# Four paired groups (two chunks of one batch each) instead of two, with a new order of work, in a linear-attention kernel with a feed-forward layer behind it

## The chip, the cores and the metric

The kernel runs on one core of one Trainium2 chip. The metric is the device time of one execution in microseconds (us), lower is better. The core has five engines that work side by side and meet only at semaphores: TensorE (PE; its weight loads are listed as PEld), VectorE (DVE), ScalarE (ACT), GpSimd (POOL) and SyncE (SP), which here does nothing but issue DMA. Data moves between HBM and SBUF (128 partitions) through 16 DMA engines, which all queues share. Matmuls write PSUM, which has 8 banks here taken two at a time as four slots.

## The reference

Two layers, one behind the other. The first is a linear attention with a state that decays; the second a feed-forward layer whose activation is a smoothed relu:

```python
# r, k, v: [4 batches, 8 heads, 768 tokens, 48];  w, u: [8, 48]
for t in range(S):
    cur = einsum('bhd,bhe->bhde', u * k[t], v[t])
    y[t] = einsum('bhd,bhde->bhe', r[t], state + cur)
    state = w * state + einsum('bhd,bhe->bhde', k[t], v[t])
x = y as [3072 tokens, 384]
h = x @ w_in                      # [3072, 2048]
g = where(h >= 1, h, where(h <= -1, 0, (h + 1)**2 / 4))
out = g @ w_out                   # [3072, 384], float32
```

## The kernel before

The 768 tokens of a batch are cut into 6 chunks of 128. The work comes in 12 **groups** of 256 tokens. Before, a group is one chunk of two batches: group g has chunk g // 2 of batches 0, 1 (g even) or 2, 3 (g odd). Two layouts exist (`PAIRED`, line 22). A **plain** group (2 to 11) has one token in each of the 128 partitions, and the two batches stand one behind the other in the free dimension; a load of its R, K or V is one DMA whose pieces are 48 numbers, 192 bytes (line 212). A **paired** group (0 and 1) has one batch in partitions 0 to 63 and the other in 64 to 127, two neighbouring tokens in a partition; its pieces are 96 numbers, 384 bytes, and a load is two DMAs of 64 partitions each (lines 203 to 207).

What one group goes through, by the names of its steps:

- `ldR`, `ldK`, `ldV`: the loads, 384 KB each; SP issues them, or ACT where the step says `@A`.
- `Rs`, `Ks` (line 289): R and K times a table of powers of w, in bf16. `T`, `TT` transpose the result on TensorE and copy it out of PSUM (for groups below `T_BY_DMA`); for the others `RK` (line 343) does it as a DMA transpose on SP's queue.
- `A` (the products of K and R within a chunk), `AT` (times a causal mask), `Vc` (V in bf16), `Y` (A times V, plus the state times R when there is an earlier chunk).
- `KU`, `RU`, `us`, `ud`: the token's own term with u, and `y`, its sum with Y.
- `Sp`, `Tm`, `dc`, `sb`: the chunk's share of the state, its sum with the old state, the decay, and the state's bf16 copy for the next chunk.
- `X`, `xT`: y transposed, on TensorE (groups below `X_BY_DMA`) or by a DMA transpose on SP's queue (line 475).
- `up` q (q = 0 to 3): 12 matmuls for a quarter of the hidden layer; `re`, `sq` on ACT and `ga` on VectorE are its activation; `dn` j, q: the matmuls of the second product for half j of the group; `o` and `st` copy it out of PSUM and store it.
- Once: `wu`, `wd`, `vu`, `vd` (tables), `wi`, `wo` (each half of w_in and w_out, issued by POOL and cast to bf16 by the DMA), `kw` n (n matmuls on zeros), `mk` (line 267, a DMA that reads the end of w_in and writes a few bytes, so SP's queue waits there for w_in).

The order is written out by hand, or rather by a search, as one list (`ORDER`, lines 29 to 65). A step with `@A`, `@D` or `@P` runs on ACT, VectorE or POOL, `#n` names the PSUM slot. The loop at line 530 issues the steps in the order of the list; each engine runs its own in that order, and an engine whose next instruction must wait holds back all that stand behind it. Work tiles have a fixed number of buffers (line 99): three each for R, K and V, two for o, KU and RU.

## Time and profile before

| | us |
|---|---|
| median of 2 runs | 206.17 (205.96 to 206.37) |
| profiled execution, its own time | 205.72 |
| its span | 203.9 |
| TensorE busy | 170.5 |
| VectorE busy | 153.8 |
| ACT busy | 126.0 |
| POOL busy | 104.1 |

The page tells busy time per engine and, in 40 slices of the span, how busy each was. The windows give the same for any stretch, with TensorE's granted clock, the share that the DMA engines were busy (above 1 where transfers overlap within an engine) and GB/s moved. The chain of waits follows the work that ended last back to its start. The timeline lists instructions with the idle time of their engine before them and what ended it.

### The profile page before, as it was taken

What the parts mean: (1) busy time and instruction counts of PE and PEld (TensorE: products, weight loads), DVE (VectorE), ACT (ScalarE), POOL (GpSimd) and SP (SyncE); (2) the same over time, 40 slices, a digit from 0 to 9 for tenths busy, and PEclk for the clock granted to TensorE, in tenths of its full rate; (3) what the DMA queues carried; (4) which work ended last, traced back from release to release, by engine and by line L of the source; (5) the groups of instructions that cost most, each with busy time, mean ns of one, the idle gap of its engine ahead of it and who ended that gap; (6) DMA issues with size and microseconds to landing.
All of it is one profiled execution on the core that took longest, in us unless ns stands there. A gap on an engine that the chain in (4) does not pass through costs nothing.

```text
span 203.9 us, 4261 instructions
## 1 busy us (share of the span) xinstructions
PE 170.5 (84%) x1780; PEld 126.5 (62%) x1780; DVE 153.8 (75%) x155; ACT 126.0 (62%) x142; POOL 104.1 (51%) x76
## 2 busy tenths in 40 slices
...
DMA  4999999993099999999999989962704710332004
GB/s 94 210 207 221 169 194 203 165 204 43 7 202 187 151 240 149 238 186 197 152 255 192 228 182 193 216 150 51 141 3 89 219 30 0 102 21 77 3 0 154
DMA packets 100452, 29.19 MB, mean 143 GB/s; under 512 B 94544, under 2 KB 99408, under 8 KB 100432
## 3 DMA queue, kind: packets, MB, share of 16 engines
...
q10 hardware_dynamic: 1056, 0.39, 0.9%
...
q14 instruction: 6, 0.05, 0.1%
HBM read 20.84 MB, written 4.72 MB: 125 GB/s over the span
## 4 chain that ended last, share of the span: by engine, by line
PE 39%; DMA 27%; DVE 9%; POOL 9%; SPq 5%; issue 5%; ACT 4%; DVEq 0%; POOLq 0%; ACTq 0%
PE hp L482 17%; PE op L504 15%; DMA V<-in_v_dram 9%; DMA RKT<-RK 7%; DMA R<-in_r_dram 6%; DMA K<-in_k_dram 5%; POOL RK L289 4%; DVE gt L497 3%; DVE KU L298 3%; SPq L207 2%; POOL RU L304 2%; PE A L366 2%; POOL V L317 1%; DVE RK L289 1%; SPq L212 1%
## 5 line engine op out<-in xcount | busy, mean ns | idle before, releaser
L482 PE MATMUL hp<-xT,w_in_sb 128*128 128x256 bf16 x576 | 72.0, 280 | 9.6 <-DVE gt L497 5.9
L489 ACT ACTIVATE pt<-hp 128x1024 f32<-128x1024 f32 x48 | 48.8, 1019 | 39.1 <-PE hp L482 38.9
L504 PE MATMUL op<-w_out_sb,gt 128*128 128x384 bf16 x384 | 69.5, 326 | 4.0 <-DVE o L117 2.5
L482 PEld LDWEIGHTS <-w_in_sb 128*128 128x128 bf16 x576 | 56.8, 100 | 21.8 <-issue 10.3
L497 DVE SCALAR_TENSOR_TENSOR gt<-sq,hp 128x1024 bf16<-128x1024 f32 x48 | 57.8, 1214 | 13.0 <-ACT sq L493 12.9
L493 ACT ACTIVATE sq<-pt 128x1024 f32<-128x1024 f32 x48 | 50.5, 1057 | 5.4 <-DVE gt L497 4.1
L504 PEld LDWEIGHTS <-gt 128*128 128x128 bf16 x384 | 35.7, 98 | 25.9 <-issue 4.1
L317 POOL TENSOR_TENSOR V<-Vb,us 128x768 f32<-128x768 bf16 (+1 forms) x11 | 14.9, 1364 | 38.7 <-DVE us L310 23.4
L378 DVE TENSOR_TENSOR AT<-A,mask 128x1024 bf16<-128x1024 f32 x20 | 24.1, 1218 | 6.9 <-PE A L366 6.9
L304 POOL TENSOR_TENSOR RU<-R,KU 128x768 f32<-128x768 f32 (+1 forms) x11 | 20.6, 1873 | 0.3
L298 POOL TENSOR_TENSOR KU<-K,u_bc 128x768 f32<-128x768 f32 (+1 forms) x9 | 14.7, 1636 | 11.8 <-DMA K<-in_k_dram 11.8
L289 POOL TENSOR_TENSOR RK<-R,W 128x768 bf16<-128x768 f32 x9 | 16.7, 1858 | 6.7 <-DMA R<-in_r_dram 6.7
L289 POOL TENSOR_TENSOR RK<-K,W 128x768 bf16<-128x768 f32 x9 | 17.4, 1932 | 2.8 <-DMA K<-in_k_dram 2.8
L329 PE MATMUL T<-ident,RK 128*128 128x128 bf16 x48 | 6.1, 293 | 9.5 <-ACT RKT L117 5.3
L412 POOL TENSOR_TENSOR state<-Tm,wCm 128x768 f32<-128x768 f32 x6 | 10.9, 1821 | 5.0 <-DVE Tm L405 5.0
L460 DVE TENSOR_TENSOR y<-Y,V 128x768 bf16<-128x768 f32 (+1 forms) x13 | 11.5, 888 | 1.7 <-PE Y L440 0.9
L310 DVE TENSOR_REDUCE us<-RU 128x16 f32<-128x768 f32 (+1 forms) x13 | 11.4, 881 | 1.0 <-POOL RU L304 1.0
L298 DVE TENSOR_TENSOR KU<-K,u_bc 128x768 f32<-128x768 f32 x4 | 9.8, 2445 | 2.3 <-DMA K<-in_k_dram 2.3
L117 ACT COPY o<-op 128x384 f32<-128x384 f32 x16 | 7.1, 480 | 7.1 <-PE op L504 7.1
L329 PEld LDWEIGHTS <-RK 128*128 128x128 bf16 x48 | 4.5, 131 | 11.0 <-issue 5.3
L117 ACT COPY RKT<-T 128x1024 bf16<-128x1024 bf16 x5 | 5.1, 1011 | 9.5 <-PE T L329 9.5
L366 PE MATMUL A<-RKT 48*128 48x128 bf16 x160 | 7.6, 218 | 3.6 <-DMA RKT<-RK 2.2
...
## 6 DMA issues: line engine op xcount, KB each, us to landing
...
```

What stands on the lines that cost most here:

```text
L117: nc.scalar.copy(out, in_) if e == "A" else engines[e].tensor_copy(out, in_)
L289: engines[e].tensor_mul(RK[g % NB][:, x, :, hs, :D], rows(got(what, g), g)[:, :, hs], table(x, g, hs))
L298: engines[e].tensor_mul(got("KU", g)[:, :, hs], rows(got("K", g), g)[:, :, hs], u_row)
L304: engines[e].tensor_mul(got("RU", g)[:, :, hs], rows(got("R", g), g)[:, :, hs], got("KU", g)[:, :, hs])
L317: engines[e].tensor_mul(got("V2", g)[:, :, hs], got("Vb", g)[:, :, hs], sums)
L366: nc.tensor.matmul(A[:, i, p, :], t[ps, 1, h, p], t[ps, 0, h, p], start=True, stop=True)
L378: nc.vector.tensor_mul(t.rearrange("p i n t -> p (i n) t"), got("A", g, h).rearrange("p i n t -> p (i n) t"), mask)
L482: nc.tensor.matmul(hp[:, f].rearrange("p (j t) -> p j t", j=2), w_in_sb[:, i, n0 : n0 + P], got("xT", g)[:, :, i, :], start=(i == 0), stop ...
L489: nc.scalar.activation(t, got("hp", g, q), AF.Relu, bias=0.5, scale=0.5)
L493: nc.scalar.activation(t, got("pt", g, q), AF.Square)
L497: nc.vector.scalar_tensor_tensor(out=t, in0=got("sq", g, q), scalar=1.0, in1=got("hp", g, q), op0=ALU.min, op1=ALU.max)
L504: nc.tensor.matmul(got("op", g)[:, j, :DO], got("gt", g, q)[:, f, j * P : (j + 1) * P], w_out_sb[:, n, :], start=(n == 0), stop=(n == nF - 1),
```

## The change

- `PAIRED` becomes groups 0 to 3, and a paired group is something else: **chunks 0 and 1 of one batch** (group g is batch g), chunk 0 in partitions 0 to 63, chunk 1 in 64 to 127, two tokens per partition as before. A load is one DMA into 128 partitions with 384-byte pieces. Groups 4 to 11 are what they were.
- Within a paired group chunk 1 needs the state of chunk 0: `Ta` (VectorE) and `sa` (a copy) make it between Sp and Y, and Y has 8 more matmuls. `Tm`, `dc`, `sb` of these groups work on one batch, half the size.
- Groups 2 and 3 have 16 + 16 short matmuls in A and 64 in Y, as groups 0 and 1 have now. Group 3 is transposed on TensorE instead of by DMA (`T_BY_DMA`, `X_BY_DMA` 3 to 4).
- The store of groups 0 to 3 is one DMA instead of two.
- R0 and K0 are both issued by ACT; `mk` is gone from the list; the whole list is new. POOL has 11 KU (9 before), 9 RU (11), 10 Ks (9), 9 dc (6), 6 sb (0) and one sa; VectorE 2 KU (4), 4 RU (2), 3 Ks (4), 1 dc (2) and 4 Ta; ACT 4 sb (10), 3 sa, 18 o (16).

SP's new list begins: ub, ldK1, ldR1, ldV0, ldR2, ldK2, ldV1, ldV2, ldR3, ldK3, ldK4, ldV3, ldK5, ldR4, ldV4, ldR5, ldV5, RK4, RK5, st0. Of the old list and of the new one the diff shows the first lines.

```diff
--- before.py
+++ after.py
@@ -19,49 +19,51 @@
 
 
 
-PAIRED = (0, 1)
+
+PAIRED = (0, 1, 2, 3)
 
 HALVED = (0,)
-T_BY_DMA, X_BY_DMA = 3, 3
+T_BY_DMA, X_BY_DMA = 4, 4
 
 
 
 ORDER = """
-ub ldK0@A tb ln lp wu0 wu1 wd1 kw21#0 lc#0 wd0 vu ldR0 Rs0.0@D KU0.0@P Ks0.0@D KU0.1@P ldK1 kw14#1 T0.0#1 ldR1 Rs0.1@D
-RU0.0@D ldV0 ldV1 Ks0.1@D wi0 us0.0 vd RU0.1@P wc kw10#0 T0.1#2 TT0.0@A TT0.1@A A0.0#3 Rs1@D Ks1@P wi1 Vc0@A Vc1@A
-ud0.0@P kw10#0 A0.1#0 T1.0#1 us0.1 ud0.1@P Sp0#2 AT0.0 Y0.0#3 AT0.1 Y0.1#0 KU1@P wo0 y0.0 y0.1 TT1.0@A Tm0 T1.1#1 mk0
-TT1.1@A kw3#3 X0#3 xT0@D A1.0#0 RU1@P A1.1#2 up0.0#1 re0.0 sq0.0 AT1.0 AT1.1 Sp1#3 us1 ud1@P Tm1 up0.1#0 Y1#2 up0.2#3
-re0.1 sq0.1 ldK2 ga0.0 up0.3#1 re0.2 sq0.2 ldR2 y1 wo1 X1#2 ga0.1 dn0.0.0#0 dn0.0.1 xT1@D up1.0#2 re0.3 ga0.2 up1.1#3
-sq0.3 KU2@D re1.0 dn0.1.0 dn0.1.1 ldK3 RU2@D sq1.0 ga0.3 ga1.0 re1.1 Rs2@P sq1.1 up1.2#1 us2 Ks2@P T2.0#2 TT2.0@D
...
+ldR0@A ldK0@A tb ln lp wu0 wu1 wd1 kw26#0 lc#0 wc vu wd0 Rs0.0@D Rs0.1@P Ks0.0@D Ks0.1@D kw10#1 T0.0#1 TT0.0@A ub
+KU0.0@P RU0.0@D us0.0 T0.1#2 TT0.1@A ldK1 KU0.1@P RU0.1@D ldR1 Rs1@D Ks1@P wi0 wi1 kw14#0 A0.0#3 AT0.0 ldV0 Vc0@A ldR2
+ud0.0@D ldK2 KU1@D ldV1 ldV2 kw11#0 T1.0#0 Sp0#1 Ta0 us0.1 Tm0 vd T1.1#2 TT1.0@A sa0@A TT1.1@A A0.1#3 A1.0#0 AT0.1
+AT1.0 Y0.0#1 y0.0 Rs2@P Ks2@P kw12#2 T2.0#2 Y0.1#3 A1.1#0 T2.1#1 TT2.0@A A2.0#2 ud0.1@D y0.1 X0#3 ldR3 AT1.1 AT2.0 wo0
+Vc1@A TT2.1@A Sp1#0 A2.1#1 RU1@P KU2@P ldK3 ldK4 Ta1 Tm1 dc0@P xT0@A up0.0#3 Vc2@A ldV3 RU2@P us1 ldK5 ldR4 sa1@A
+dc1@P sb0@A re0.0 sq0.0 ldV4 ldR5 Sp2#2 Ta2 Tm2 up0.1#0 AT2.1 ga0.0 Y1#2 up0.2#1 sa2@A re0.1 sq0.1 sb1@A ud1@P y1 X1#3
+Rs3@P us2 re0.2 sq0.2 xT1@D up0.3#2 re0.3 up1.0#3 ga0.1 ga0.2 Ks3@P T3.0#0 TT3.0@D sq0.3 ga0.3 Y2#1 ud2@P y2 re1.0
+sq1.0 ga1.0 up1.1#0 dc2@P wo1 A3.0#2 AT3.0 re1.1 sq1.1 ga1.1 X2#1 up1.2#3 xT2@A KU3@P T3.1#2 TT3.1@D Vc3@P Sp3#1 Ta3
+Tm3 re1.2 sq1.2 ga1.2 up1.3#0 re1.3 sq1.3 KU4@P sb2@P A3.1#2 AT3.1 ga1.3 up2.0#1 re2.0 sq2.0 up2.1#3 re2.1 sq2.1 RU3@P
+us3 ga2.0 dn0.0.0#2 dn0.1.0 sa3@P Y3#0 dc3@P Vc4@A sb3@A dn0.1.1 up2.2#1 RU4@P ud3@P y3 X3#0 dn0.0.1 ga2.1 xT3@D Rs4@D
+us4 KU5@P RU5@D up2.3#3 up3.0#0 dn0.0.2 dn0.1.2 dn0.0.3 dn0.1.3 re2.2 sq2.2 ga2.2 us5 dn1.0.0#1 dn1.1.0 ldV5 dn1.0.1
...
+st11.1
 """
 
 
@@ -184,6 +186,15 @@
         return x.rearrange("p h d -> p (h d)")
 
 
+    def place(g):
+
+        if g in PAIRED:
+            return 0, g // 2, []
+        if g < 4:
+            return g - 2, 1, [2] if g > 2 else []
+        c, bp = 2 + (g - 4) // 2, g % 2
+        return c, bp, [g - 2] if c > 2 else [2 * bp, 2 * bp + 1] if 2 * bp in PAIRED else [3]
+
     def heads(g, part):
 
         if part is None:
@@ -197,26 +208,21 @@
     def table(i, g, hs):
         return W2[i][:, :, hs] if g in PAIRED else W1[i][:, hs].unsqueeze(1).to_broadcast([P, 2, hs.stop - hs.start, D])
 
-    def load(queue, tile_, x, g, part):
-        c, bp = divmod(g, BP)
-        hs, _ = heads(g, part)
-        if g in PAIRED:
-            for i in range(2):
-                src = x[bp * 2 + i, hs, c * C : (c + 1) * C, :].rearrange("h (q e) d -> q h (e d)", e=2)
-                dst = tile_[i * HP : (i + 1) * HP].rearrange("p (h e) d -> p h (e d)", e=2)[:, hs]
-                queue.dma_start(out=dst, in_=src)
-        else:
-            src = x[bp * 2 : bp * 2 + 2, hs, c * C : (c + 1) * C, :].rearrange("b h t d -> t b h d")
-            dst = tile_.rearrange("p (b h) d -> p b h d", b=2)[:, :, hs]
-            assert part is None
-            queue.dma_start(out=tile_, in_=src.rearrange("t b h d -> t (b h) d"))
+    def load(queue, tile_, x, g):
+        c, bp, _ = place(g)
+        if g in PAIRED:
+            src = x[g, :, : 2 * C, :].rearrange("h (p e) d -> p h (e d)", e=2)
+            queue.dma_start(out=tile_.rearrange("p (h e) d -> p h (e d)", e=2), in_=src)
+        else:
+            src = x[bp * 2 : bp * 2 + 2, :, c * C : (c + 1) * C, :]
+            queue.dma_start(out=tile_, in_=src.rearrange("b h t d -> t (b h) d"))
 
 
     def step_tb(e, s):
         nc.scalar.preload_act_table_set("natural_log_exp_and_others")
 
     def step_ub(e, s):
-        nc.sync.dma_start(out=u_bc, in_=bcast(u))
+        (nc.scalar if e == "A" else nc.sync).dma_start(out=u_bc, in_=bcast(u))
 
     def step_ln(e, s):
         nc.scalar.activation(lw, w_bc, AF.Ln)
@@ -264,7 +270,7 @@
         nc.gpsimd.dma_start(out=w_out_sb[:, n, :], in_=w_out_src[:, n, :])
 
     def step_mk(e, s, i):
-        nc.sync.dma_start(out=mark, in_=(w_in_sb[:1, nK - 1, DF - 16 :],)[i])
+        nc.sync.dma_start(out=mark, in_=w_in_sb[:1, 0, :16])
 
     def step_kw(e, s, n):
         t = bank(s, "idle", (), [P, P], F32)
@@ -272,10 +278,8 @@
             nc.tensor.matmul(t, warm, warm, start=True, stop=True, skip_group_check=True)
 
     def loader(what, x):
-        def step(e, s, g, part=None):
-            if heads(g, part)[1]:
-                new(what, (g,), [P, 2 * H, D], F32)
-            load(nc.scalar if e == "A" else nc.sync, got(what, g), x, g, part)
+        def step(e, s, g):
+            load(nc.scalar if e == "A" else nc.sync, new(what, (g,), [P, 2 * H, D], F32), x, g)
 
         return step
 
@@ -397,25 +401,37 @@
                         flat(got("Vb", g)[:, j, hs, :]), start=True, stop=True, skip_group_check=True,
                     )
 
+    def state_of(g, x):
+        c, bp, _ = place(g)
+        return x[bp][:, g % 2] if g in PAIRED else x[bp]
+
+    def step_Ta(e, s, g):
+        nc.vector.tensor_mul(flat(state_of(g, states)), got("Sp", g)[:, 0, :DM], flat(wCm))
+
+    def step_sa(e, s, g):
+        copy(e, state_of(g, states_bf), state_of(g, states))
+
     def step_Tm(e, s, g):
-        c, bp = divmod(g, BP)
         Sp = got("Sp", g)[:, :, :DM]
-        if c:
+        S = state_of(g, states)
+        if g in PAIRED:
+            t = new("Tm", (g,), [P, NP, 2 * D], F32)
+            nc.vector.tensor_add(flat(t), Sp[:, 1], flat(S))
+        elif place(g)[2]:
             t = new("Tm", (g,), [P, 2, NP, 2 * D], F32)
-            nc.vector.tensor_add(t.rearrange("p j n d -> p j (n d)"), Sp, states[bp].rearrange("p j n d -> p j (n d)"))
-        else:
-            wc = wCm.rearrange("p n d -> p (n d)").unsqueeze(1).to_broadcast([P, 2, DM])
-            nc.vector.tensor_mul(states[bp].rearrange("p j n d -> p j (n d)"), Sp, wc)
+            nc.vector.tensor_add(t.rearrange("p j n d -> p j (n d)"), Sp, S.rearrange("p j n d -> p j (n d)"))
+        else:
+            nc.vector.tensor_mul(S.rearrange("p j n d -> p j (n d)"), Sp, flat(wCm).unsqueeze(1).to_broadcast([P, 2, DM]))
 
     def step_dc(e, s, g):
-        wc = wCm.unsqueeze(1).to_broadcast([P, 2, NP, 2 * D])
-        engines[e].tensor_mul(states[g % BP], got("Tm", g), wc)
-
-    def step_sb(e, s, g):
-        copy(e, states_bf[g % BP], states[g % BP])
+        wc = wCm if g in PAIRED else wCm.unsqueeze(1).to_broadcast([P, 2, NP, 2 * D])
+        engines[e].tensor_mul(state_of(g, states), got("Tm", g), wc)
+
+    step_sb = step_sa
 
     def step_Y(e, s, g, part=None):
-        c, bp = divmod(g, BP)
+        S = state_of(g, states_bf)
+        goes_on = place(g)[2]
         hs, _ = heads(g, part)
         h0 = hs.start
         Y = bank(s, "Y", (g, part), [P, 2, 512], F32)
@@ -423,13 +439,9 @@
         for p in range(h0 // 2, hs.stop // 2):
             cols = slice((2 * p - h0) * D, (2 * p + 2 - h0) * D)
             if g in PAIRED:
-                if c:
-                    for f in range(2):
-                        for un in range(2):
-                            q = slice(un * HP, (un + 1) * HP)
-                            nc.tensor.matmul(
-                                Y[q, f, cols], t[:, 0, f, p, q], states_bf[bp][:, un, p, :], start=True, stop=False, skip_group_check=True
-                            )
+                q = slice(HP, 2 * HP)
+                for f in range(2):
+                    nc.tensor.matmul(Y[q, f, cols], t[:, 0, f, p, q], S[:, p, :], start=True, stop=False, skip_group_check=True)
                 AT = got("AT", g, p // 2)
                 for i in range(2):
                     h = 2 * p + i
@@ -439,17 +451,17 @@
                                 q = slice(un * HP, (un + 1) * HP)
                                 nc.tensor.matmul(
                                     Y[q, f, (h - h0) * D : (h + 1 - h0) * D], AT[q, i, p % 2, e2, f * HP : (f + 1) * HP], V[q, e2, h, :],
-                                    start=(c == 0 and e2 == 0), stop=(e2 == 1), skip_group_check=True,
+                                    start=(un == 0 and e2 == 0), stop=(e2 == 1), skip_group_check=True,
                                 )
             else:
                 for j in range(2):
-                    if c:
-                        nc.tensor.matmul(Y[:, j, cols], t[:, 0, j, p, :], states_bf[bp][:, j, p, :], start=True, stop=False, skip_group_check=True)
+                    if goes_on:
+                        nc.tensor.matmul(Y[:, j, cols], t[:, 0, j, p, :], S[:, j, p, :], start=True, stop=False, skip_group_check=True)
                     for i in range(2):
                         h = 2 * p + i
                         nc.tensor.matmul(
                             Y[:, j, (h - h0) * D : (h + 1 - h0) * D], got("AT", g, j)[:, i, p, :], V[:, j, h, :],
-                            start=(c == 0), stop=True, skip_group_check=True,
+                            start=not goes_on, stop=True, skip_group_check=True,
                         )
 
     def step_y(e, s, g, part=None):
@@ -512,13 +524,12 @@
         copy(e, got("o", g)[:, j], got("op", g)[:, j, :DO])
 
     def step_st(e, s, g, j=None):
-        c, bp = divmod(g, BP)
+        c, bp, _ = place(g)
         o = got("o", g)
         r0 = bp * 2 * S + c * C
         if g in PAIRED:
-            for i in range(2):
-                dst = out[r0 + i * S : r0 + i * S + C, :].rearrange("(q e) d -> q (e d)", e=2)
-                nc.sync.dma_start(out=dst, in_=o[i * HP : (i + 1) * HP].rearrange("p e d -> p (e d)"))
+            dst = out[g * S : g * S + 2 * C, :].rearrange("(p e) d -> p e d", e=2)
+            nc.sync.dma_start(out=dst, in_=o)
         elif j is None:
             dst = bass.AP(tensor=out.tensor, offset=out.offset + r0 * DO, ap=[[DO, C], [S * DO, 2], [1, DO]])
             nc.sync.dma_start(out=dst, in_=o)
```

## Rows read from the trace of the kernel before

**Rows 1.** The page: span, TensorE's busy time, DMA's busy tenths in 40 slices.
```profile
span 203.9 us, 4261 instructions
...
PE 170.5 (84%) x1780; PEld 126.5 (62%) x1780; DVE 153.8 (75%) x155; ACT 126.0 (62%) x142; POOL 104.1 (51%) x76
...
DMA  4999999993099999999999989962704710332004
```

**Rows 2.** Windows by stage: length, busy us (instructions) per engine, clock, DMA share, GB/s.
```profile
29.97:51.00 21.03, 16.52 (x199) 13.09 (x198) 18.70 (x15) 13.15 (x13) 11.26 (x7) 0.92 0.97 152
51.00:130.00 79.00, 67.60 (x698) 48.65 (x697) 67.57 (x62) 51.99 (x61) 57.27 (x34) 0.98 1.15 184
130.00:200.50 70.50, 69.01 (x641) 50.16 (x639) 51.07 (x49) 50.30 (x55) 20.50 (x13) 1.00 0.34 77
```

**Rows 3.** The chain that ended last: start us, us, what; landmarks.
```profile
11.94 12.98 DMA V<-in_v_dram
...
29.97 1.49 PE hp L482 x12
...
76.19 6.71 DMA RKT<-RK
...
200.53 0.48 ACT o L117
```

**Rows 4.** Windows of single stretches, columns as in rows 2.
```profile
0.00:5.00 5.00, 2.42 (x21) 2.16 (x21) 2.77 (x15) 1.92 (x3) 2.35 (x12) 1.00 0.48 92
...
10.00:11.00 1.00, 0.00 (x0) 0.00 (x0) 0.58 (x2) 0.00 (x0) 1.00 (x2) 1.00 1.34 204
...
6.00:7.00 1.00, 1.00 (x6) 1.00 (x6) 0.60 (x2) 1.00 (x3) 0.00 (x0) 1.00 1.22 257
...
47.00:56.00 9.00, 8.76 (x74) 6.19 (x74) 7.20 (x9) 6.23 (x8) 0.00 (x0) 0.81 0.03 5
65.00:66.00 1.00, 1.00 (x10) 0.71 (x8) 0.92 (x1) 0.00 (x0) 0.92 (x2) 1.00 1.45 187
```

**Rows 5.** Waits of SP's queue: waiter, releaser: us in total, times, longest us.
```profile
SPq L343 <- DVE RK L289: 15.7, 2, 10.4
...
SPq L267 <- DMA w_in_sb<-in_moe_w_in_dram: 11.6, 1, 11.6
```

**Rows 6.** The chain that ended last: prices of TensorE's steps.
```profile
33.33 1.12 PE Y L440 x64
...
53.15 0.46 PE T L329 x8
...
153.47 2.62 PE hp L482 x24
...
165.52 0.33 PE A L366 x8
...
193.84 5.21 PE op L504 x32
```

**Rows 7.** Timeline: start us, us, engine, line, op, out<-in, [idle before <-releaser].
```profile
39.18 5.88 DVE L298 TENSOR_TENSOR KU<-K,u_bc 128x768 f32<-128x768 f32 x1
...
67.59 0.95 DVE L298 TENSOR_TENSOR KU<-K,u_bc 128x768 f32<-128x768 f32 x1
...
42.45 1.79 POOL L304 TENSOR_TENSOR RU<-R,KU 128x768 f32<-128x768 f32 x1
...
47.24 2.72 PE L482 MATMUL hp<-xT,w_in_sb 128*128 128x256 bf16 x12 [4.51 <-DVE gt L497]
...
58.12 0.21 PE L447 MATMUL Y<-state_bf,RKT 128*128 128x96 bf16 x1
...
58.86 2.11 PE L504 MATMUL op<-w_out_sb,gt 128*128 128x384 bf16 x12
```

**Rows 8.** Timeline of ACT: the two passes over one quarter of the hidden layer.
```profile
33.52 1.00 ACT L489 ACTIVATE pt<-hp 128x1024 f32<-128x1024 f32 x1
34.55 1.06 ACT L493 ACTIVATE sq<-pt 128x1024 f32<-128x1024 f32 x1
```

70 lines of the change are left out of this document (35 added, 35 removed).

## The prediction

> **What bounds the kernel now.** I read the page first. In a span of 203.9 us TensorE is busy 170.5 us, more than any other engine, and the DMA row reads 9 from about 5 to 45 us, drops to 0 near 50 and fills again until about 125 [rows 1]. An average over such different stages says little, so the busy time by stages comes next. From the first feed-forward matmul (29.97 us, [rows 3]) to 51 us TensorE is busy 16.5 of 21.0 us; from 51 to 130 us 67.6 of 79.0; from 130 to 200.5 us 69.0 of 70.5 [rows 2]. The reader is to see three kernels: a start in which almost no feed-forward work can run, a middle that loses time all the way, and an end that TensorE alone sets. Only start and middle can be shortened.
>
> What is late there is told by the chain that ended last. Before the first feed-forward matmul it passes through V of group 1, 12.98 us from issue to landing; in the middle it goes through DMA again and again, as in the 6.71 us of a DMA transpose [rows 3]. The moved bytes say why the start is slow. While SP's loads into 64 partitions run alone, they move 204 GB/s (10 to 11 us); later the 192-byte pieces into all 128 partitions move 187 (65 to 66 us); the best is 257, at 6 to 7 us, when ACT's K for one half of the partitions and SP's R for the other are in flight together [rows 4]. And from 47 to 56 us 5 GB/s are moved [rows 4]: SP waits, once 11.6 us in the marker for w_in and twice, 15.7 us together, in a DMA transpose for a product of VectorE [rows 5]. Groups 4 to 11 are loaded only after that.
>
> **TensorE's work, as a base.** A feed-forward quarter up takes 1.31 us (2.62 for two), one down matmul 0.163 (5.21 for 32) [rows 6]: 48 x 1.31 = 62.9 and 384 x 0.163 = 62.5. Attention: twenty plain A halves at 0.33 and four paired at some 0.5 (16 short matmuls for 8; bounds 0.33 and 0.66) 8.6; T six times 0.46, 2.8; X three times 0.35 (six transposes for T's eight), 1.1; paired Y twice 1.12 [rows 6], plain Y ten times 0.74 (from 58.12 to 58.86, [rows 7]), 9.6; Sp ten times some 0.35 (eight matmuls as in T, a quarter narrower), 3.6 with the paired ones. Together 151.1. Ahead of the first up stand T of groups 0 and 1 (1.8), their A (2.0), Sp0 (0.4), Y0 (1.1), X0 (0.35): 5.7. So 145.4 remain, and from 29.97 to the last matmul's end at 200.5 there are 170.5 us: **25 us lost**. Of these the windows show 4.5 + 11.4 + 1.5 = 17.4 as idle [rows 2]; the rest is matmuls run at the lower clock (mean granted clock 0.92 from 30 to 51) or held up within a group. From 200.5 to the span's end at 203.9 come the last copy and store, 3.4 us.
>
> **The change, part by part.**
>
> *Added TensorE work.* Groups 2 and 3 become paired: four A halves at +0.17 (0.7); Y of groups 2 and 3 from 0.74 to 1.12 + 8 state matmuls at some 0.05, +0.75 each; Y of 0 and 1 +0.37 each (2.2); Sp +0.2. Group 3 is now transposed on TensorE: T twice 0.46, X 0.35. Sum 4.4: 155.5 in all. Bounds: A and Sp free, 3.3; each doubled, 5.3. Nothing hides this, since TensorE sets the end.
>
> *Loads of the first four groups.* Twelve loads of 393 kB (128 x 768 x 4 bytes). Before, six go in 64-partition halves at 204 GB/s and six in 192-byte pieces at 187: 11.6 + 12.6 = 24.2 us of transfer. After, all twelve are 384-byte pieces into 128 partitions. No row shows such a load. The lower bound is 204 (pieces set the pace, no gain from more partitions), the upper 257, seen with both halves in flight [rows 4]; I take 257, for it is the same pieces to all the partitions: 18.4 us, 6 us saved. The Trainium skill, "SBUF — State Buffer", Door 1: The DMA port swizzle, says that partitions 0 to 63 reach 8 of 16 ports (196 GB/s for 1 MiB) and 0 to 127 all (328). Its 196 is near the row's 204; by its 328 the loads would take 14.4 us, 4 us less again, which no row here shows.
>
> *When the first up starts.* In the new TensorE order it stands behind T, A of groups 0, 1 and 2 and Sp1, and ACT's first relu behind the cast of V2. So w, u, nine loads and w_in must come first: 0.39 + 3.54 + 1.57 = 5.5 MB. By 5 us 0.46 MB are in (92 GB/s, [rows 4]). Of the rest w_in takes 1.57/0.204 = 7.7 us, the other 3.47 MB 13.5 us at 257: V2 lands at 26.2 us (29.7 at 204). The first up does not need V2, but needs K2, two POOL products of 1.8 us [rows 7], T2 and A2 behind it; I put it at **27.5** (25.5 to 31). By then TensorE has done 8.5 us (T 2.8, A 3.0, Y0 1.5, X0 0.35, Sp 0.9), not 5.7; 147.0 remain.
>
> *The marker and the waits of SP go.* By bytes R3, K3, V3 and w_out (1.57 MB) are then in by 26.2 + 4.6 + 7.7 = 38.5 us, where before the DMA row is full until 47. And SP's list now has K4, K5, R4, V4, R5, V5 before its first DMA transpose, so it does not stand in one from 44 to 55. Groups 4 and on are loaded some 18 us sooner (38.5 for 56), as far as three buffers each allow. That is where I expect most of the gain: the 11.4 idle us from 51 to 130.
>
> *Moved between engines.* Full-size products of two SBUF tensors on VectorE fall from about 16.5 to 13.5; POOL gains about 7 us (state copies, two KU more, one Ks more, the halved dc). POOL's list from Rs2 to KU5 (twelve products at 1.8 us, three ud at 1.5, four half dc at 0.9, copies, w_out's two issues) is some 33 us back to back: from 16 to 49 us, and y3 needs ud3 near its end. ACT loses most state copies. The four Ta and sa (half size, under 0.6 us each) put Sp, VectorE and ACT ahead of each of the first four Y; TensorE has A of the next group, warm-up or ups to run meanwhile, so I cost them at nothing; bare, they would be some 1.5 us per group, 6 us in all.
>
> *What is left as loss.* Ten ups come before the first down. ACT needs 1.00 + 1.06 us for each [rows 8], and some 2.5 us for copies: 23 us, against 19 us of TensorE work there. Loss 4.5. From there to 130 us: at least 2 (the end's rate of 1.5 in 70 us), at most the old 11.4 idle plus the 6 us held within groups; I take 7, nearer the low end since the loads are ahead. 1.5 in the end. **13 us.**
>
> **Sum.** 27.5 + 147.0 + 13 + 3.4 = 190.9 us of span. Around the span of the profiled execution lay 205.72 - 203.9 = 1.8 us, and 205.72 stands 0.45 under the median, 206.17: **193 us** (192.7; ratio 0.935).
>
> **The rivals.**
>
> *Little of the middle's loss goes (A).* The chain there also holds POOL, and POOL's work grows by 7 us. If POOL paces groups 4 to 8 and the loads only wait in their buffers, the loss stays at 20 to 25: 198 to 205. For it: the old middle has POOL at 57 of 79 us [rows 2]. Against: much of its idle time was waiting for loads.
>
> *The loads are no faster (B).* 204 GB/s for 384-byte pieces: the first up at 31, V2 at 29.7 and its cast stalling ACT; loss 15: 31 + 147 + 15 + 3.4 + 1.8 = 198. For it: the 257 was seen for one us only.
>
> *VectorE starves beside POOL (C), the other side.* K times u on VectorE started at 39.18 us and took 5.88 us, while three POOL products ran back to back, the last from 42.45 to 44.24 [rows 7]; it ended 0.82 us after that. Undisturbed it takes 0.95 (at 67.59). The event cost 4.9 us of VectorE, and TensorE stood 4.51 us behind the gate product after it [rows 7]. The Trainium skill, "SBUF — State Buffer", Who interferes with whom, has such a product wait for GpSimd's instruction under way (an exclusive lock); by it alone 1.8 us would be lost, the row shows three times that. Now POOL is back to back for 33 us, with K1 times u, Rs4 and RU5 on VectorE in or just behind it. One event is within my loss; from three fully exposed on (193 + 3 x 4.9 = 208) the change gives nothing, and with four it is slower, 212. Against: VectorE has fewer such products than before, and elsewhere in this trace they waited for one POOL product, not for three.
>
> **Chances and range.** My forecast (187 to 197) 0.5; A 0.2, of which a quarter ends above 202; B 0.13; C 0.17, of which 0.05 stays within 2%. A measurement tells about 2% from no change: under 202.0 is faster, above 210.3 slower. Faster: 0.5 + 0.15 + 0.12 = 0.77, less 0.1 for an order whose waits I followed closely only to 60 us: 0.67. Same: 0.05 + 0.01 + 0.05 + 0.08 = 0.19. Slower: 0.14. The range for 8 in 10 runs from 187 (loss 7) to 207 (A whole, C in part); the forecast's own is 187 to 197.
>
> **What would show it.** Right: a window at 8 to 12 us at 240 GB/s or more; first up between 25.5 and 31 us; no hole in the DMA row between 40 and 56; loads of group 4 landing before 50; TensorE idle at most 8 us from 51 to 130. Wrong: 205 GB/s there (B); the DMA row full early, but the middle's idle time as before, with POOL as releaser (A); VectorE products of 4 us or more (C); ACT sitting in the cast of V2 beyond 30 us.

## The result and the profile after

The changed kernel takes **197.57 us** (197.56 to 197.58, two runs) where the kernel before took 206.17 (205.96 to 206.37): ratio 0.9583, 95% interval 0.9542 to 0.9624. It is faster by 8.6 us; 193 was forecast, with 187 to 207 as the range. The profiled execution took 197.58 with a span of 195.8.

On the three chips of the experiments below, executions of the kernel before spread from 201.3 to 207.9 us (and one took 426), and the ratios there take of each kernel only those within 1.5% of its fastest. By that measure the changed kernel's ratio on one of these chips is 0.9781 (0.971 to 0.9853, e11_after_again), a gain of 4.4 us. That it is faster is shown; how much, between 4.4 and 8.6 us, is not settled.

From the page of the changed kernel: span, TensorE's busy time, its granted clock and the DMA engines in 40 slices (beside [rows 1]).

```profile
span 195.8 us, 4641 instructions
...
PE 176.3 (90%) x1977; PEld 132.1 (67%) x1977; DVE 149.2 (76%) x156; ACT 124.0 (63%) x142; POOL 116.6 (60%) x88
...
PEclk9999559999999999999999999999999999999998
DMA  4999999899900597869953949975869953121022
```

TensorE does more and is busier. The DMA row is full early, as forecast, but the hole is still there: it moved from the tenth and eleventh slice to the twelfth and thirteenth, 54 to 64 us (its first 2 us lie in the 40 to 56 that the forecast named). And the clock falls from about 20 to 30 us. Windows of the changed kernel, columns as in [rows 2]: two of the loads, then the three stages.

```profile
8.00:12.00 4.00, 2.50 (x21) 1.74 (x18) 2.16 (x4) 1.55 (x4) 1.76 (x2) 1.00 1.22 259
12.00:18.00 6.00, 3.96 (x45) 3.33 (x45) 5.96 (x5) 2.83 (x4) 5.98 (x5) 1.00 1.13 258
33.33:51.00 17.67, 17.48 (x304) 14.31 (x305) 16.34 (x20) 15.60 (x19) 15.88 (x12) 1.00 1.12 186
51.00:130.00 79.00, 74.91 (x782) 54.99 (x778) 64.06 (x63) 54.08 (x60) 60.35 (x40) 1.00 0.70 141
130.00:192.10 62.10, 60.60 (x562) 43.41 (x560) 42.56 (x40) 40.29 (x45) 19.44 (x13) 1.00 0.51 107
```

TensorE's idle time from the first feed-forward matmul to 51 us fell from 4.5 to 0.2 us, from 51 to 130 us from 11.4 to 4.1, and in the end it stayed at 1.5 [rows 2]. Against that, the first feed-forward matmul starts later than before: at 33.33 us in the chain (33.26 in the timeline) instead of 29.97 [rows 3]. What it waited for, in the chain of the changed kernel up to there (start us, us, what):

```profile
1.21 8.89 DMA K<-in_k_dram
...
15.31 5.74 DVE RK L293
...
26.80 1.41 PE idle L278 x12
...
33.33 1.42 PE hp L494 x12
```

The one piece of over 2 us that is not a load is a VectorE product, R of group 1 times the powers of w (`Rs1`), of 5.74 us. The timeline of the three engines around it, POOL, VectorE and TensorE (columns as in [rows 7]):

```profile
12.85 2.12 POOL L293 TENSOR_TENSOR RK<-K,W 128x768 bf16<-128x768 f32 x1
14.92 1.71 POOL L266 DMA_DIRECT2D w_in_sb<-in_moe_w_in_dram  x2
16.66 1.81 POOL L293 TENSOR_TENSOR RK<-R,W 128x768 bf16<-128x768 f32 x1
18.42 1.80 POOL L293 TENSOR_TENSOR RK<-K,W 128x768 bf16<-128x768 f32 x1
...
15.31 5.74 DVE L293 TENSOR_TENSOR RK<-R,W 128x768 bf16<-128x768 f32 x1
...
21.11 1.04 PE L333 MATMUL T<-ident,RK 128*128 128x128 bf16 x8 [5.07 <-DVE RK L293]
```

`Rs1` starts while POOL issues w_in, and ends 0.83 us after POOL's second product behind that issue (18.42 + 1.80 = 20.22; 15.31 + 5.74 = 21.05). TensorE stands idle for 5.07 us, and from 20 to 30 us its granted clock is 0.50, the lower of its two levels: twelve idle matmuls there take 1.41 us in the chain.

### The profile page after: what moved, and what is told of

Same layout as the page of the kernel before. It is cut to its first block, busy times and chain, and to the rows that moved or that the text cites. A ratio compares the mean times of both kernels' runs of the same rounds, so it can differ in the third digit from the quotient of the medians.

```text
span 195.8 us, 4641 instructions
## 1 busy us (share of the span) xinstructions
PE 176.3 (90%) x1977; PEld 132.1 (67%) x1977; DVE 149.2 (76%) x156; ACT 124.0 (63%) x142; POOL 116.6 (60%) x88
## 4 chain that ended last, share of the span: by engine, by line
PE 59%; DVE 19%; DMA 8%; ACT 6%; issue 5%; POOL 1%; SPq 0%; ACTq 0%; DVEq 0%
PE op L516 24%; PE hp L494 23%; DVE RK L293 5%; DMA K<-in_k_dram 5%; DVE gt L509 5%; PE Y L452 3%; DMA R<-in_r_dram 3%; ACT sq L505 2%; ACT pt L501 2%; DVE RU L308 2%; PE A L370 2%; PE Y L444 2%; DVE us L314 2%; ACT o L119 1%; POOL RU L308 1%
## 5 line engine op out<-in xcount | busy, mean ns | idle before, releaser
L494 PE MATMUL hp<-xT,w_in_sb 128*128 128x256 bf16 x576 | 69.9, 273 | 1.5 <-DVE gt L509 1.4
L494 PEld LDWEIGHTS <-w_in_sb 128*128 128x128 bf16 x576 | 55.0, 98 | 11.9 <-DVE gt L509 1.6
L321 POOL TENSOR_TENSOR V<-Vb,us 128x768 f32<-128x768 bf16 x11 | 16.9, 1539 | 13.8 <-DVE Vb L119 10.0
L382 DVE TENSOR_TENSOR AT<-A,mask 128x1024 bf16<-128x1024 f32 x16 | 19.1, 1217 | 5.1 <-PE A L370 5.0
L308 POOL TENSOR_TENSOR RU<-R,KU 128x768 f32<-128x768 f32 x9 | 17.9, 1992 | 5.4 <-DVE KU L302 5.2
L302 POOL TENSOR_TENSOR KU<-K,u_bc 128x768 f32<-128x768 f32 (+1 forms) x11 | 19.0, 1728 | 3.6 <-DMA K<-in_k_dram 3.6
L293 POOL TENSOR_TENSOR RK<-K,W 128x768 bf16<-128x768 f32 x10 | 19.2, 1922 | 0.0
L428 POOL TENSOR_TENSOR state<-Tm,wCm 128x768 f32<-128x768 f32 (+1 forms) x9 | 13.1, 1451 | 9.1 <-DVE Tm L419 4.7
L293 POOL TENSOR_TENSOR RK<-R,W 128x768 bf16<-128x768 f32 (+1 forms) x9 | 15.6, 1737 | 3.6 <-DMA R<-in_r_dram 3.6
L314 DVE TENSOR_REDUCE us<-RU 128x16 f32<-128x768 f32 (+1 forms) x13 | 11.4, 881 | 0.5 <-POOL RU L308 0.5
L293 DVE TENSOR_TENSOR RK<-R,W 128x768 bf16<-128x768 f32 (+1 forms) x4 | 11.4, 2848 | 0.0
L119 POOL CAST Vb<-V 128x768 bf16<-128x768 f32 x6 | 4.9, 821 | 8.4 <-DMA V<-in_v_dram 8.4
```

What stands on the lines that cost most here:

```text
L119: nc.scalar.copy(out, in_) if e == "A" else engines[e].tensor_copy(out, in_)
L293: engines[e].tensor_mul(RK[g % NB][:, x, :, hs, :D], rows(got(what, g), g)[:, :, hs], table(x, g, hs))
L302: engines[e].tensor_mul(got("KU", g)[:, :, hs], rows(got("K", g), g)[:, :, hs], u_row)
L308: engines[e].tensor_mul(got("RU", g)[:, :, hs], rows(got("R", g), g)[:, :, hs], got("KU", g)[:, :, hs])
L314: nc.vector.tensor_reduce(got("us", g)[:, :, hs], got("RU", g)[:, :, hs], AX.X, ALU.add)
L321: engines[e].tensor_mul(got("V2", g)[:, :, hs], got("Vb", g)[:, :, hs], sums)
```

## The experiments

Single executions of one kernel spread by 0.8 to 5.4 us here, so each run has its median (of all executions) with the lowest and highest, and the ratio to the kernel before on the same chip, taken as said above. Runs with one number of a chip shared that chip and one set of times of the kernel before. "First up" is the start of the first feed-forward matmul in the timeline of the profiled execution.

| | chip | median (lowest to highest) us | ratio, 95% interval | span | first up |
|---|---|---|---|---|---|
| e1_rs1_pool | 13 | 198.32 (197.81 to 198.93) | 0.9757 (0.9626 to 0.9888) | 196.3 | 33.99 |
| e2_half_loads | 13 | 198.44 (198.07 to 199.53) | 0.977 (0.9632 to 0.9909) | 197.8 | 35.38 |
| e3_paired01 | 13 | 195.56 (195.05 to 195.83) | 0.9612 (0.944 to 0.9784) | 194.0 | 32.72 |
| e5_late_loads | 13 | 202.1 (199.55 to 203.94) | 0.9892 (0.9806 to 0.9978) | 199.7 | 31.37 |
| e7_ru1_first | 8 | 194.84 (192.8 to 195.18) | 0.9635 (0.9582 to 0.9688) | 191.0 | 28.55 |
| e8_paired01_ru1 | 8 | 193.49 (191.38 to 196.74) | 0.9485 (0.9346 to 0.9624) | 189.6 | 28.23 |
| e4_before_vc1 | 8 | 201.1 (198.6 to 203.54) | 0.9899 (0.9719 to 1.0078) | 199.6 | 23.62 |
| e10_before_vc1_products | 12 | 201.2 (197.25 to 202.59) | 0.9824 (0.9697 to 0.995) | 195.4 | 24.29 |
| e11_after_again | 12 | 197.84 (196.27 to 199.2) | 0.9781 (0.971 to 0.9853) | 197.4 | 34.92 |
| e12_paired01_cast | 12 | 197.23 (195.0 to 198.78) | 0.9719 (0.9649 to 0.979) | 195.8 | 30.56 |
| e13_ru1_again | 12 | 194.92 (192.97 to 195.5) | 0.962 (0.9559 to 0.9681) | 193.4 | 30.86 |
| e14_ru1_fill | 8, later | 194.23 (194.0 to 194.98) | 0.961 (from one execution of the kernel before) | 193.1 | 30.46 |

### The starved product moved to POOL (e1_rs1_pool)

```diff
-... ldR1 Rs1@D Ks1@P wi0 ...
+... ldR1 Rs1@P Ks1@P wi0 ...
```

> One token moved: the product Rs1 runs on POOL, ahead of Ks1, instead of on VectorE, where it took 5.74 us beside POOL's products. Theory 1 (this starved product made the start late): T of group 1 starts at about 16 us instead of 21.1, the granted clock does not stand at 0.5 from 20 to 30 us, the first up starts at 27 to 29 instead of 33.3, and the time falls by 3 to 5 us, to 192.5 to 194.5. Theory 2 (the loads of V1, V2 and w_in set the first up anyway): the first up moves by at most 1.5 us, the time stays at 196 to 197.6. Theory 3 (POOL, with one more product ahead of w_in's issue, becomes late): 197.6 or more.

The first up came at 33.99 us, not earlier. VectorE's and POOL's timeline in this run:

```profile
17.20 5.74 DVE L302 TENSOR_TENSOR KU<-K,u_bc 128x768 f32<-128x768 f32 x1
...
16.80 1.71 POOL L266 DMA_DIRECT2D w_in_sb<-in_moe_w_in_dram  x2
18.54 1.82 POOL L293 TENSOR_TENSOR RK<-R,W 128x768 bf16<-128x768 f32 x1
20.30 1.81 POOL L293 TENSOR_TENSOR RK<-K,W 128x768 bf16<-128x768 f32 x1
```

The next VectorE product of that size, K1 times u, took the same 5.74 us beside the same three steps of POOL and ended 0.83 us after them (22.94 to 22.11). TensorE stood 5.59 us behind it:

```profile
24.48 0.34 PE L444 MATMUL Y<-state_bf,RKT 128*64 128x96 bf16 x2 [5.59 <-DVE Tm L419]
```

So it is not this product that is slow: whichever starts there waits. The run does not tell what on POOL it waits for.

### What POOL has ready (e7_ru1_first, e13_ru1_again beside e11_after_again)

`RU1` needs K1 times u from VectorE. Put ahead of group 2's two products in POOL's list, it holds them back until VectorE is through.

```diff
-... y0.0 Rs2@P Ks2@P kw12#2 ... A2.1#1 RU1@P KU2@P ...
+... y0.0 RU1@P Rs2@P Ks2@P kw12#2 ... A2.1#1 KU2@P ...
```

> One token of the new order moved: POOL does RU1 ahead of Rs2 and Ks2. RU1 needs KU1 from VectorE, so behind w_in's issue POOL has nothing ready that reads SBUF, and VectorE gets through. Theory 1 (VectorE's product starves only while POOL's next product is already ready): Rs1 and KU1 take under 1.7 us each instead of 5.74 for one of them, T of group 1 starts at 16 to 17.5 us, the clock is at 0.5 for under 4 us, the first up starts at 28 to 30.5, and the time falls by 2 to 4.5 us, to 193 to 195.5. Theory 2 (the start is bound by POOL's and the loads' sum, and the starvation only fills a gap, as it seemed when Rs1 went to POOL): first up at 32 to 34, time 197 to 198.5.

The timeline of e7_ru1_first, VectorE, POOL, TensorE:

```profile
15.53 0.94 DVE L293 TENSOR_TENSOR RK<-R,W 128x768 bf16<-128x768 f32 x1
...
17.99 0.94 DVE L302 TENSOR_TENSOR KU<-K,u_bc 128x768 f32<-128x768 f32 x1
...
15.13 1.71 POOL L266 DMA_DIRECT2D w_in_sb<-in_moe_w_in_dram  x2
19.03 1.81 POOL L308 TENSOR_TENSOR RU<-R,KU 128x768 f32<-128x768 f32 x1 [2.19 <-DVE KU L302]
...
24.43 0.40 PE L333 MATMUL T<-ident,RK 128*128 128x128 bf16 x4 [1.37 <-POOL RK L293]
...
28.55 1.48 PE L494 MATMUL hp<-xT,w_in_sb 128*128 128x256 bf16 x12
```

`Rs1` starts during the issue of w_in as before, but takes 0.94 us, and so does K1 times u. POOL now waits 2.19 us, and TensorE later 1.37 us for POOL's product of K2, which comes later for it; that costs less than it saves. The first up comes 4.7 us sooner than in the changed kernel, and the span is 4.8 us shorter (191.0 to 195.8): in this pair what the start gains passes to the end whole. The median is 194.84 us. Because the chips differ, both kernels then ran on one:

> The changed kernel as it is, to stand beside the next ones on the same chip: 197.2 to 198, span 195.8, first feed-forward matmul near 33.3 us, granted clock 0.5 from 20 to 30 us.

> The changed kernel with R1's product ahead of group 2's products on GpSimd (as e7_ru1_first), beside the changed kernel itself on the same chip. If the gain of e7_ru1_first is real: 193 to 195, 2 to 4 us under e11_after_again, first feed-forward matmul near 28.5 us. If it was the chip's spread: within 1 us of it.

197.84 and 194.92 us, ratios 0.9781 and 0.962 with intervals that do not touch; first up 34.92 and 30.86, 4.06 us apart, spans 4.0 apart. The gain is real.

e7_ru1_first and e13_ru1_again are one kernel, with first ups 2.3 us apart. The work is the same; what differs is the clock. The window from 20 to 30 us, of e7_ru1_first:

```profile
20.00:30.00 10.00, 7.70 (x184) 5.97 (x186) 8.76 (x11) 5.73 (x8) 9.81 (x7) 1.00 1.12 215
```

and of e13_ru1_again:

```profile
20.00:30.00 10.00, 8.93 (x150) 7.03 (x152) 7.72 (x8) 4.11 (x6) 9.95 (x7) 0.55 1.13 218
```

At a granted clock of 0.55 the same work is behind by 2.3 us at the first up and by 2.4 in the span. The eleven executions of this kernel fit: the two with a mean clock of 0.999 took 192.8 and 192.97 us, the one with 0.986 took 193.62, and those between 0.94 and 0.971 took 194.79 to 195.5, in no order among themselves.

### Gaps filled with idle matmuls (e14_ru1_fill)

```diff
-... wd1 kw26#0 lc#0 ... kw10#1 T0.0#1 TT0.0@A ub
+... wd1 kw43#0 lc#0 ... kw14#1 T0.0#1 TT0.0@A kw12#3 ub
-AT1.0 Y0.0#1 ...
+kw12#2 AT1.0 Y0.0#1 ...
```

> e7_ru1_first with idle matmuls in three gaps of TensorE before the feed-forward part: 43 instead of 26 in the gap from 4 to 6 us, 14 instead of 10 and 12 more around the first transposes, 12 more behind group 1's A. Where e7_ru1_first's profiled execution kept the granted clock at 1.00 it had the first feed-forward matmul at 28.55 us and a span of 191.0 us; where e13_ru1_again, the same kernel, fell to 0.50 after 2.0 idle us at 4 us and again near 20 us, these were 30.86 and 193.4. Theory: the clock falls because TensorE idles, and costs 2.3 us that pass to the end; with the gaps filled it stays at 1.00: first feed-forward matmul at 28.3 to 28.8 us, 192.5 to 193.5 us. Rival: it falls all the same (it is not these gaps), and the added matmuls at half speed delay the transposes of group 2: first one at 31 us or later, 195 to 196.

194.23 us, between the two. The gaps at 4 to 6 us and around the first transposes are filled and the clock stays 1.00 to 20 us (0.62 from 5 to 15 in e13_ru1_again), but then it falls again. TensorE's timeline:

```profile
20.83 1.44 PE L278 MATMUL idle<-warm 128*128 128x128 bf16 x12 [2.20 <-ACT RKT L119]
```

My third filler waited itself, 2.20 us, for ACT to empty its PSUM slot, and ran at half speed in front of work that was ready. So the third gap was not filled, and the run can't say whether the clock would have held. That idle time alone brings the fall is not shown either: in e7_ru1_first TensorE idled the same 2.0 us at 4 us and kept its clock. The six executions of this version lie within 1 us (those of e7_ru1_first on that chip within 2.4), below all of the kernel before there (202.2 and more; only that one enters the ratio); the changed kernel did not run there.

### Loads in halves (e2_half_loads)

```diff
-            src = x[g, :, : 2 * C, :].rearrange("h (p e) d -> p h (e d)", e=2)
-            queue.dma_start(out=tile_.rearrange("p (h e) d -> p h (e d)", e=2), in_=src)
+            for i in range(2):
+                src = x[g, :, i * C : (i + 1) * C, :].rearrange("h (p e) d -> p h (e d)", e=2)
+                queue.dma_start(out=tile_[i * HP : (i + 1) * HP].rearrange("p (h e) d -> p h (e d)", e=2), in_=src)
```

> Only the loads of groups 0 to 3 change: each is two DMAs of 64 partitions with the same 384-byte pieces. If writing all 128 partitions is what raised the rate, the windows from 8 to 14 us fall from about 258 to about 204 GB/s, K0's first product starts 1 to 2 us later, the first up 1 to 3 us later, and the time is 198.5 to 200.5. If the rate comes from something else (two queues, no marker), windows and time stay: 197.2 to 198.

The same pieces and order, in two DMAs of 64 partitions for each load. Its windows:

```profile
8.00:12.00 4.00, 1.00 (x8) 0.47 (x6) 0.56 (x1) 0.84 (x2) 1.37 (x1) 0.50 1.33 197
12.00:18.00 6.00, 4.37 (x50) 3.75 (x51) 5.19 (x6) 3.37 (x4) 5.19 (x4) 0.50 1.32 205
```

197 and 205 GB/s, where the changed kernel has 259 and 258, and the old one 204 [rows 4]: the 128 partitions do it, not the length of a piece. The first up came 2.1 us later and the span is 2.0 longer, but here the clock was 0.50 from 8 to 18 us as well; in the median it stands 0.1 us from e1_rs1_pool on the same chip. That is no ceiling for the faster loads, because VectorE's wait changed too. Its timeline:

```profile
17.89 0.95 DVE L294 TENSOR_TENSOR RK<-R,W 128x768 bf16<-128x768 f32 x1
...
19.89 3.35 DVE L322 TENSOR_TENSOR V<-Vb,us 128x384 f32<-128x384 bf16 x1
```

`Rs1` took 0.95 us here (why, e3_paired01 shows below); the product that waited was `ud0.0`, 3.35 us where it took 0.54 in the changed kernel, so the wait was 2.8 us and not 4.8. VectorE's first product of K0 started 2.6 us later (12.78 for 10.20). So in this order the faster loads show 2 us at the first up; what they are worth where nothing waits beside POOL was not run.

### Two paired groups instead of four (e3_paired01, e8_paired01_ru1)

```diff
-PAIRED = (0, 1, 2, 3)
+PAIRED = (0, 1)
...
-... Sp2#2 Ta2 Tm2 ... sa2@A ... dc2@P ... Sp3#1 Ta3 ... sa3@P ...
+... Sp2#2 Tm2 ...
```

> Same order, but only groups 0 and 1 are paired; groups 2 and 3 are plain (chunks 0 and 1 of batches 2 and 3, one token per partition, 192-byte pieces), without their extra state steps. TensorE's work is smaller by about 2.7 us, six loads take some 3.4 us more of DMA time in all (187 for 257 GB/s). If the start is set by VectorE and not by the loads, the first up stays at 33 us and the time falls to 195 to 197; if the rate of groups 2 and 3 counts, the first up is 1 to 3 us later and the time 198 to 200.

TensorE is busy 172.6 us instead of 176.3, and the kernel takes 195.56 us, 2.8 less than e1_rs1_pool on the same chip. One line of its timeline was the key to e7_ru1_first:

```profile
15.40 0.94 DVE L293 TENSOR_TENSOR RK<-R,W 128x768 bf16<-128x768 f32 x1
```

Nothing was done to `Rs1`, which starts during the issue of w_in as in the changed kernel, and it takes 0.94 us. What differs is R2, which POOL's next product needs. Its DMA, in the view of the transfers issued from 8.3 to 9.4 us (KB, us from issue to landing), in the changed kernel, where it is issued at 8.57:

```profile
R<-in_r_dram SPq DMA_DIRECT2D x1, 384.0 KB, 6.6
```

and in e3_paired01, where it is issued at 8.82 and its pieces are shorter:

```profile
R<-in_r_dram SPq DMA_DIRECT2D x1, 384.0 KB, 6.7
```

So R2 lands at 15.17, 0.14 us ahead of `Rs1` (15.31), in the one, and at 15.52, 0.12 us behind it (15.40), in the other (the view gives the way to landing to 0.1 us). With POOL's next product ready, VectorE's waits; without, it runs. The other runs with this order of POOL agree: R2 landed 0.15 us ahead of `Rs1` in e11_after_again and e5_late_loads, which took 5.74 and 5.75 us; in e2_half_loads its second half, issued at 11.9, landed 6.2 us later or more, some 0.2 us behind the start, and `Rs1` took 0.95. K1 times u then meets POOL's `Ks2` in e3_paired01 and takes 2.55 us.

> The same move of RU1 in the version in which only groups 0 and 1 are paired. Theory 1: KU1, which took 2.55 us there, and ud0.0, 1.59, fall to 0.95 and 0.54; first up at 28 to 31 instead of 32.7; 192 to 194.5, less than both kernels. Theory 2: no change, 195 to 196.

With POOL's order of e7_ru1_first it takes 193.49 us, and the span 189.6, against 194.84 and 191.0 on the same chip at nearly the same clock (0.994 and 0.999). The intervals of the two ratios overlap. Pairing groups 2 and 3 buys nothing that these runs show; by the spans, one execution each, it costs 1.4 us.

### The cast of V2 later (e12_paired01_cast)

In e8_paired01_ru1 TensorE waits 1.50 us behind the first up for ACT's cast of V2:

```profile
31.20 0.50 PE L399 MATMUL Sp<-Vb,RK 128*128 128x96 bf16 x8 [1.50 <-ACT Vb L119]
```

```diff
-... up0.0#3 Vc2@A ldV3 ... re0.0 sq0.0 ldV4 ldR5 Sp2#2 Tm2 up0.1#0 ...
+... up0.0#3 ldV3 ... re0.0 sq0.0 Vc2@A ldV4 ldR5 up0.1#0 Sp2#2 Tm2 ...
```

> e8_paired01_ru1 (groups 0 and 1 paired alone, R1's product ahead of group 2's products on GpSimd), with ACT's cast of V2 behind the first relu and square, and a second feed-forward quarter ahead of Sp2 on TensorE. Theory: the 1.50 us that TensorE waited for the cast of V2 behind the first feed-forward quarter, and part of the .62 us at 44, are a wait on ACT's list, not on the load; they go: 191 to 193. Rival: the wait only moves to the second quarter or to Sp2, since ACT has the same amount of work up to there: no change, 193 to 194.

197.23 us, 2.3 more than e13_ru1_again on its chip. TensorE's timeline:

```profile
36.07 0.50 PE L399 MATMUL Sp<-Vb,RK 128*128 128x96 bf16 x8 [1.61 <-ACT Vb L119]
37.62 0.24 PE L444 MATMUL Y<-state_bf,RKT 128*64 128x96 bf16 x2 [1.05 <-DVE state L424]
```

The wait went behind the second quarter, as the rival had it, and a second one came with it: Sp2 later makes the state later. The edit was wrong; it did not run on one chip with e8_paired01_ru1, so its price is not measured.

### Group 5 loaded late (e5_late_loads)

```diff
-... us1 ldK5 ldR4 ... ldV4 ldR5 ... ldV5 ...
+... us1 ldR4 ... ldV4 ... y3 mk3 ldK5 ldR5 ldV5 ...
```

with `mk` reading a few bytes of y3, so that SP waits there as it did before the change.

> K5, R5, V5 are loaded only after y of group 3 (60 us): SP waits there with a marker DMA, as it stood in a wait until 56 us in the kernel before. If the loads being ahead removed the middle's loss, POOL's KU5 (58.5 us) starts some 6 to 8 us later, TensorE's idle time from 51 to 130 us rises from 4 us to 8 to 12, and the time is 201 to 206. If the new order alone brought it, the time stays within 1 us of 197.6.

202.1 us is the median of ten executions; the five that enter the ratio have 201.26, 2.9 more than e1_rs1_pool on the same chip, and all ten (199.55 and more) lie above all four of e1_rs1_pool (198.93 and less). That is so though its first up was 2.6 us sooner: `Rs1` waited as in the changed kernel, but the clock was back at 1.00 from 26 us. Group 5's loads are issued from 59.7 us; its timeline, VectorE, POOL and TensorE, shows who waits:

```profile
15.30 5.75 DVE L293 TENSOR_TENSOR RK<-R,W 128x768 bf16<-128x768 f32 x1
...
64.28 1.81 POOL L302 TENSOR_TENSOR KU<-K,u_bc 128x768 f32<-128x768 f32 x1 [7.09 <-DMA K<-in_k_dram]
...
69.85 4.00 PE L516 MATMUL op<-w_out_sb,gt 128*128 128x384 bf16 x12 [3.70 <-DVE gt L509]
```

and its window of the middle what it costs: 6.84 us idle (8 to 12 were expected), and a clock of 0.96, where the changed kernel has 4.1 and 1.00:

```profile
51.00:130.00 79.00, 72.16 (x734) 52.30 (x732) 57.86 (x56) 50.09 (x56) 57.29 (x37) 0.96 0.75 144
```

One group of three loads late gives back some 2.9 us, where e1_rs1_pool stands 4.9 below the kernel before by its ratio.

### The old order with one step moved (e4_before_vc1, e10_before_vc1_products)

In the kernel before, ACT waited 6.76 us for V1 in front of the transposes' copies that the first up needs:

```profile
25.00 0.83 ACT L117 CAST Vb<-V 128x768 bf16<-128x768 f32 x1 [6.76 <-DMA V<-in_v_dram]
```

```diff
-... Vc0@A Vc1@A ... TT1.1@A kw3#3 ...
+... Vc0@A ... TT1.1@A Vc1@A kw3#3 ...
```

> The kernel before with one token moved: ACT casts V1 only after both copies of group 1's transposes, so it no longer holds them while V1 is under way (until 25 us). If the late start of the kernel before cost what it seemed to, the first up starts at 25 to 27 us instead of 30 and the time falls by 2 to 4.5 us, to 201.5 to 204 where the kernel before has 206. If the middle, whose loads come no earlier, takes the gain back, the first up is earlier and the time stays within 1 us.

The first up comes at 23.62 us, 6.3 sooner, and the median is 201.1. By the ratio, 0.9899, some 2 us were to be had in the old layout with one step moved, and its interval, 0.9719 to 1.0078, does not exclude none; by that most of the earlier start is lost again behind it. Its timeline shows the next wait, VectorE's, then TensorE's:

```profile
34.60 0.95 DVE L298 TENSOR_TENSOR KU<-K,u_bc 128x768 f32<-128x768 f32 x1
38.82 2.60 DVE L304 TENSOR_TENSOR RU<-R,KU 128x768 f32<-128x768 f32 x1 [3.27 <-DMA R<-in_r_dram]
...
42.60 2.72 PE L482 MATMUL hp<-xT,w_in_sb 128*128 128x256 bf16 x12 [4.46 <-DVE gt L497]
```

> The kernel before, with the cast of V1 moved behind the last transpose copy of group 1 (as in e4_before_vc1) and two of VectorE's products, K2 times u and R2's product behind it, put on GpSimd. Theory: in e4_before_vc1 the feed-forward work starts at 23.6 us, but K2 times u on VectorE still stands 5.9 us beside GpSimd's run and TensorE idles 4.46 us behind it; with both products on GpSimd no VectorE product starts beside a ready run there, and some 4 us of this come back: 195 to 198. Rival: groups 4 and on are still loaded only from 56 us, and GpSimd gets 3.6 us more to do, so the gain is given back in the middle: 200 to 202, the idle time from 51 to 130 us as large as in e4_before_vc1 (11 us) or larger.

This expectation had the event of [rows 7] in mind and misread this trace: K2's product takes 0.95 us here, and what held VectorE was R2's load (3.27 us) and 2.60 us beside POOL. With both products on POOL the stand of 4.46 us is gone and the profiled execution, the fastest of six, has a span of 195.4; but the median stays at 201.2, with 10.3 us idle from 51 to 130 us (11.0 in e4_before_vc1). The intervals of the two ratios overlap; whether this helps is not settled.

## Why the prediction was right, and where it was not

The sum was 27.5 + 147.0 + 13 + 3.4 = 190.9 us of span. Measured: 33.3 + 147.0 + 11.8 + 3.7 = 195.8, with the 147.0 taken over. The direction and the main mechanism were right, one term was not. Of the 13 us of gain that were forecast, 8.6 came, or 4.4 by the ratio on the chip of e11_after_again.

**TensorE's added work, right as far as can be seen.** 4.4 us were forecast; busy time rose by 5.8 [rows 1], of which the fifteen idle matmuls added (73 for 58) are 1 to 1.8. The clock moves busy time as well (176.3 in the changed kernel, 172.9 in e7_ru1_first with the same work), so this is a rough check.

**The load rate, right; rival B falls.** 259 GB/s from 8 to 12 us for the 257 taken. The Trainium skill, "SBUF — State Buffer", Door 1: The DMA port swizzle, has 196 GB/s for 64 partitions and 328 for 128, both for 1 MiB. The direction agrees with 197 and 259 here; 328 did not come with these short pieces.

**The first up, wrong: 33.3 for 27.5, outside 25.5 to 31.** This is the step that failed. It priced bytes, POOL products and TensorE, and left out a VectorE product that waits beside POOL. That was rival C's mechanism, with the right price, 5.74 - 0.94 = 4.8 us for 4.9, but at a place not among those named (K1 times u, Rs4, RU5), and not "within my loss": ahead of the first up it adds in full. Without it the first up is at 28.55 us at full clock, one us from the forecast, and at 30.86 with a fallen one, within the bounds both times (e7_ru1_first, e13_ru1_again); with it 33.26 and 34.92, and 31.37 in e5_late_loads, where the clock rose again soonest. So the clock, which the sum did not have either, moves the first up by 2 to 3.5 us on top. And there is luck in the one us: V2, forecast for 26.2 us, landed at some 20 (issued at 13.5, 6.4 us to landing), and what then came last, in the chain of e7_ru1_first, was POOL's product of K2 (until 24.38), not a load. Behind the first up C hardly returned: the longest such product there takes 2.55 us (below).

**The marker and the loads ahead, right.** SP's timeline, the loads of groups 4 and 5 (first and last of the six):

```profile
23.59 3.41 SPq L218 DMA_DIRECT2D K<-in_k_dram  x1
...
43.87 2.97 SPq L218 DMA_DIRECT2D V<-in_v_dram  x1
```

They are issued by 44 us. Before, R4 alone went out earlier (40.24); the next, K4, in that kernel's timeline of SP:

```profile
56.64 1.10 SPq L212 DMA_DIRECT2D K<-in_k_dram  x1
```

e5_late_loads shows that this matters. The mark "no hole in the DMA row" was badly chosen: SP stands 17.8 us in its first DMA transpose, longer than the two such waits of [rows 5] together (15.7), but no wait of TensorE in the middle is for what stands behind it.

**The loss afterwards, 11.8 for 13.** The 4.5 us for an ACT-bound stretch did not come: 0.2 us idle to 51 us, and 0.4 from 29 to 51 us in e7_ru1_first, which starts as early as forecast. I had set 23 us of ACT against 19 of TensorE; TensorE had 22.0 us of work up to the first down matmul (33.26 to 55.49 us), and ACT itself waited for it there (0.74 and 1.05 us). The middle's idle time fell to 4.1 us, within the 8 named, and rival A falls: of its four waits above 0.2 us, 4.0 us together, none is for POOL, though POOL's work grew by 12.5 us (7 were forecast). The two longest, in TensorE's timeline:

```profile
103.36 1.49 PE L494 MATMUL hp<-xT,w_in_sb 128*128 128x256 bf16 x12 [1.27 <-DVE gt L509]
...
115.62 0.81 PE L516 MATMUL op<-w_out_sb,gt 128*128 128x384 bf16 x4 [1.63 <-DVE o L119]
```

**What it did not see.** Pairing four groups is not the source of the gain: two paired groups do as well (e3_paired01, e8_paired01_ru1). The faster loads show 2 us at the first up and nothing in the median (e2_half_loads), beside a shorter wait of VectorE. That the order carries the rest is what remains, and not shown as a whole: the new order did not run on the old layout. Of the order, the loads ahead of SP's waits are shown to count (e5_late_loads); that the stand of [rows 7] is gone is seen in the trace, its share was not measured.
